# Raw weights in two pieces, later ranks behind the last mixing, rows of units asked for at any step, and a Gram rate of 1.4 in the first two mixings

## The chip, the cores and the metric

The program runs on one core of one Trainium2 chip. The metric is the device time of one execution in microseconds. The engines are named as in the profile: PE (TensorE, matmuls), PEld (its weight loads), DVE (VectorE), ACT (ScalarE), POOL (GpSimd) and SP (SyncE). SP and POOL mostly issue transfers here; "SPq" and "POOLq" are the rows in which they do so.

## What is computed

Four batches of column-normalised attention are followed by a top-1 mixture of experts over all tokens. B = 4, N = 5056, C = 256, E = 8 experts, F = 1024.

```python
qn = q / (norm(q, axis=1) + 1e-6);  kn = k / (norm(k, axis=1) + 1e-6)
s  = kn.T @ qn / tau                       # per batch: 256 x 256, summed over 5056 rows
a  = softmax(s)
x  = (v @ a).reshape(20224, 256)
e  = argmax(x @ w_gate);  p = softmax(x @ w_gate)[e]
eom = sigmoid(x @ w_output_gate)
out = p * eom[e] * (relu(x @ w1[e]) @ w2[e])   # each token by its own expert e
```

## The kernel before, in words

**Stages.** For each batch there is a *Gram* (`gram(b)`, 20 steps of 256 rows: one `qk` tile of two 256 KB loads on SP, squares on ACT L353, their sum on DVE L354, the fp32 products `s_ps` on PE L366), whose tail turns norms and products into the softmax matrix. Then comes a *mixing* (`mix(b)`, 20 turns): v is loaded on SP (L465), transposed on PE (`vt_ps` L477), split into a high and a low part (`vh` on ACT L481, `vl` on DVE L483), and multiplied by the matrix in three products (`x_ps` L506 to L508). ACT copies the result with its gate logits into a tile `st` (L509). Each group of 1024 tokens (5 groups a mixing) is *routed*: DVE finds the best expert (one-hot `r_oh` L556), PE counts by matmuls (`r_ps` L576, L579), DVE makes slot numbers (`r_si` L591), and POOL scatters the eight rows of tokens of each partition into a sorted scratch `xs_d` in DRAM, eight indirect DMAs a group (L598).

**Ranks and weights.** After two mixings the experts are ranked by how many tokens they have (`checkpoint`, whose `ri` holds the rows of rank r's weights). `prep` then loads the raw fp32 weights of each rank on SP, 1 MB for w1 (half 0, L273) and 1 MB for w2 (half 1, L276), at most DEEP = 2 halves ahead. `split` takes the root mean square of a half (ACT squares L297 and one matmul `w_ps` L301), writes fp16 high and low parts (ACT L310, DVE L311) and stores them to a scratch `wsc` (L316). Rank 0 is split right into `wbuf`. Raw tiles of ranks 0 and 1 are of their own tag "raw"; those of ranks 2 to 7 lie in the pool of `st`, four buffers that the routed rows use too, so a raw load into one waits until the scatters that read it are done.

**Units.** The expert layers run in units of 256 (later 128) slots of one expert, in order of rank: units 0 to 3 are rank 0, unit 4 is the first that may be of rank 1, unit 11 the first of rank 2. For each unit POOL fetches w1 and w2 with indirect DMAs into one of two `wbuf` slots (`fetch_w` L825, 1 MB each), SP fetches the rows (`fetch_x` L843, into the six `qk` buffers), `prepare` scales and splits them (DVE L863, ACT L880, DVE L881) and SP transposes them with two DMAs a unit (L885). PE makes h (L919 to L921, 48 matmuls), ACT and DVE split it (L923, L924), PE makes y (L942 to L944, 48 matmuls), ACT scales it (L948) and POOL scatters the rows to the output (L954). `blocks` yields after each quarter of a unit, with the y of the unit before beside the h of this one.

**What sets the order.** The program interleaves these generators by rates (`_steps`): so many steps of the second generator for each step of the first. The framework then schedules the instructions on each engine by a simulated timeline, so a changed rate, tile or number of DMAs moves instructions on every engine. Within an engine, and within SP's and POOL's issue streams, the order is fixed in the program: an instruction that waits holds up all behind it. GRATE is the number of Gram steps for each mixing step, REST the pauses before a half is split, MRATE and WRATE the steps of `prep` for each step of the last mixing and of the units behind it.

## Time and profile before

| what | value |
|---|---|
| median of 3 runs | 1206.93 us (1206.85 to 1208.63) |
| the profiled execution's own time | 1209.88 us |
| its span on the core | 1208.1 us |
| mean granted PE clock | 0.99 |
| PE, DVE, ACT, POOL busy | 1174.4, 748.5, 602.3, 517.9 us |
| HBM read, written | 281.84 MB, 61.41 MB |

The span falls into stages: Gram 0 until about 60 us, mixings 0 and 1 beside Grams 1 to 3 until about 255 us, mixing 2 beside the first units until about 355 us, the last mixing beside units until about 450 us, units alone until about 1190 us. In a view of waits a line reads "engine, instruction, what it waited for: us in all, times, longest". In a view of windows the columns are the length and then busy us and count of PE, PEld, DVE, ACT and POOL, the granted clock, the DMA share and GB/s. In a timeline the first number is the start, the second the length, and brackets hold the idle time of the engine ahead of it with what ended it. In a chain of waits each row is a start, a length and what took that time.

### The profile page before, as it was taken

The page shows a single profiled execution, that of the slowest core. Times are in us where ns is not written, and L with a number is a line of the kernel's source. Part 1 is how long each engine was busy: PE and PEld are TensorE (multiplying, and loading weights), DVE is VectorE, ACT ScalarE, POOL GpSimd, SP SyncE. Part 2 cuts the span into 40 slices and gives each one's busy share as a digit, 9 for nine tenths or more (in the row PEclk, how much of TensorE's full clock was granted, in tenths as well). Part 3 has the DMA queues.
Part 4 walks back from the last instruction along what each step waited for, and adds up shares of the span by engine and source line. Part 5 has one row for each costly group of instructions (what it writes and reads, how often), then busy time and mean ns, then how long its engine had stood idle before and what let it go on. Part 6 is the DMA issues. An engine that isn't in the chain of part 4 may idle for free.

```text
span 1208.1 us, 28097 instructions
## 1 busy us (share of the span) xinstructions
PE 1174.4 (97%) x10412; PEld 1066.4 (88%) x10412; DVE 748.5 (62%) x2300; ACT 602.3 (50%) x1193; POOL 517.9 (43%) x518
## 2 busy tenths in 40 slices
PE   8999999997997999999999999999999999999997
PEld 7899999887996888888888888888889999999997
DVE  7787768788685966566666654555554555555531
ACT  6576656576574555555556443333333444344432
POOL 0003756536565753333444433344444444444433
PEclk9999999998998999999999999999999999999999
DMA  9976888877767898657554436643325534336533
GB/s 319 330 246 207 301 277 259 295 242 215 212 242 236 223 264 178 150 147 174 148 137 126 112 80 113 182 76 77 72 63 176 112 73 82 79 81 197 168 104 130
DMA packets 186307, 208.56 MB, mean 173 GB/s; under 512 B 121832, under 2 KB 134510, under 8 KB 182200
## 3 DMA queue, kind: packets, MB, share of 16 engines
q1 hardware_dynamic: 145368, 139.41, 42.0%
q0 software_dynamic: 40512, 67.05, 18.9%
q8 instruction: 84, 1.38, 0.5%
q14 instruction: 55, 0.45, 0.1%
q10 hardware_dynamic: 288, 0.26, 0.1%
HBM read 281.84 MB, written 61.41 MB: 284 GB/s over the span
## 4 chain that ended last, share of the span: by engine, by line
PE 87%; DMA 6%; DVE 2%; issue 2%; ACT 1%; SPq 1%; POOL 0%; POOLq 0%; DVEq 0%; ACTq 0%
PE h_ps L919 11%; PE h_ps L921 11%; PE h_ps L920 11%; PE y_ps L942 11%; PE y_ps L943 11%; PE y_ps L944 11%; PE s_ps L366 10%; PE x_ps L506 3%; PE x_ps L508 2%; PE x_ps L507 2%; PE vt_ps L477 2%; DMA wbuf<-wsc,wi 1%; DMA qk<-in_k_dram 1%; DMA raw<-in_moe_w_dram 1%; DMA qk<-in_q_dram 1%
## 5 line engine op out<-in xcount | busy, mean ns | idle before, releaser
L924 DVE SCALAR_TENSOR_TENSOR hb<-h_ps,hb 128x512 f16<-128x512 f32 (+1 forms) x360 | 228.5, 636 | 276.0 <-ACT hb L923 275.1
L923 ACT ACTIVATE hb<-h_ps 128x512 f16<-128x512 f32 (+1 forms) x360 | 197.9, 552 | 364.1 <-PE h_ps L921 362.5
L919 PE MATMUL h_ps<-xt,wbuf 128*128 128x256 f16 (+1 forms) x1440 | 366.5, 262 | 3.0 <-ACT st L509 3.0
L921 PE MATMUL h_ps<-xt,wbuf 128*128 128x256 f16 (+1 forms) x1440 | 366.6, 262 | 0.0
L920 PE MATMUL h_ps<-xt,wbuf 128*128 128x256 f16 (+1 forms) x1440 | 366.5, 262 | 0.0
L942 PE MATMUL y_ps<-wbuf,hb 128*128 128x256 f16 x1296 | 353.3, 273 | 5.0 <-ACT yo L948 2.4
L944 PE MATMUL y_ps<-wbuf,hb 128*128 128x256 f16 x1296 | 353.3, 273 | 0.0
L943 PE MATMUL y_ps<-wbuf,hb 128*128 128x256 f16 x1296 | 353.3, 273 | 0.0
L825 POOL DMA_INDIRECT wbuf<-wsc,wi x172 | 177.8, 1034 | 404.5 <-PE h_ps L921 365.2
L598 POOL DMA_INDIRECT xs_d<-st,r_si x160 | 168.1, 1051 | 199.2 <-DVE r_d L550 101.9
L954 POOL DMA_INDIRECT out_dram<-yo,b_id x162 | 165.4, 1021 | 69.2 <-issue 42.3
L366 PE MATMUL s_ps<-qk 128*128 128x256 f32 x640 | 152.4, 390 | 5.8 <-DMA qk<-in_q_dram 3.9
L920 PEld LDWEIGHTS <-wbuf 128*128 128x128 f16 x1440 | 141.0, 98 | 16.9 <-issue 3.2
L919 PEld LDWEIGHTS <-wbuf 128*128 128x128 f16 x1440 | 142.1, 99 | 14.1
L921 PEld LDWEIGHTS <-wbuf 128*128 128x128 f16 x1440 | 141.1, 98 | 13.3
L943 PEld LDWEIGHTS <-hb 128*128 128x128 f16 x1296 | 126.8, 98 | 19.3 <-issue 5.6
L366 PEld LDWEIGHTS s_ps<-qk 128*128 128x128 f32 x640 | 121.4, 196 | 21.2 <-DMA qk<-in_k_dram 3.9
L944 PEld LDWEIGHTS <-hb 128*128 128x128 f16 x1296 | 126.8, 98 | 14.9
L942 PEld LDWEIGHTS <-hb 128*128 128x128 f16 x1296 | 126.8, 98 | 14.3
L354 DVE TENSOR_TENSOR acc<-acc,sq 128x1024 f32<-128x1024 f32 x76 | 92.9, 1223 | 46.8 <-ACT sq L353 45.4
L880 ACT ACTIVATE xr<-xg,b_sx 128x256 f16<-128x256 f32 x162 | 74.6, 502 | 66.8 <-DVE b_sx L233 46.4
L353 ACT ACTIVATE sq<-qk 128x1024 f32<-128x1024 f32 x76 | 80.3, 1060 | 53.0 <-DMA qk<-in_k_dram 44.8
(191 smaller groups left out, 1448.8 us busy)
## 6 DMA issues: line engine op xcount, KB each, us to landing
xg<-xs_d SPq DMA_DIRECT2D x72, 272.0 KB
qk<-in_q_dram SPq DMA_DIRECT2D x75, 256.0 KB
qk<-in_k_dram SPq DMA_DIRECT2D x75, 256.0 KB
v<-in_v_dram SPq DMA_DIRECT2D x32, 512.0 KB
raw<-in_moe_w_dram SPq DMA_DIRECT2D x16, 1024.0 KB
wsc<-whi SPq DMA_DIRECT2D x14, 512.0 KB
wsc<-wlo SPq DMA_DIRECT2D x14, 512.0 KB
v<-in_v_dram SPq DMA_DIRECT2D x8, 480.0 KB
```

What stands on the lines that cost most here:

```text
L366: nc.tensor.matmul(s_ps[:, c, :], kt[:, 1, t, c * P : (c + 1) * P], qt[:, 0, t, :], start=st == 0 and t0 == 0 and t == 0 and c == 0 and n ...
L598: ins = nc.gpsimd.indirect_dma_start(out=xs_d[:, :], out_offset=bass.IndirectOffsetOnAxis(ap=si[:np_, t : t + 1], axis=0), in_=st[:np_, t, ...
L825: nc.gpsimd.indirect_dma_start(out=wbuf[half][:, at_of(u), :], out_offset=None, in_=wsc[half][:end, :], in_offset=bass.IndirectOffsetOnAxi ...
L919: nc.tensor.matmul(hp, w1s[:, 0, c, fs], xh, start=fi == 0 and c == 0, stop=False, **KWM)
L920: nc.tensor.matmul(hp, w1s[:, 0, c, fs], xl, start=False, stop=False, **KWM)
L921: nc.tensor.matmul(hp, w1s[:, 1, c, fs], xh, start=False, stop=fin, **KWM)
L923: nc.scalar.activation(hh, h_ps[:, :, :w], AF.Relu)
L924: nc.vector.scalar_tensor_tensor(out=hb[:, 1, 2 * fp : 2 * fp + 2, :w], in0=h_ps[:, :, :w], scalar=0.0, in1=hh, op0=ALU.max, op1=ALU.subtract,
L942: nc.tensor.matmul(y_ps[:, t, :], hb[:, 0, f, tsl], w2s[:, 0, f, :], start=st, stop=False, **KWM)
L943: nc.tensor.matmul(y_ps[:, t, :], hb[:, 0, f, tsl], w2s[:, 1, f, :], start=False, stop=False, **KWM)
L944: nc.tensor.matmul(y_ps[:, t, :], hb[:, 1, f, tsl], w2s[:, 0, f, :], start=False, stop=fin, **KWM)
L954: ins = nc.gpsimd.indirect_dma_start(out=out[:, :], out_offset=bass.IndirectOffsetOnAxis(ap=un["id"][:, t : t + 1], axis=0), in_=un["yo"][ ...
```

## The change

Six things change.

1. In the first two mixings the next Grams run at 1.4 steps to a mixing step in place of 1.3 (AHEAD_RATE); the third mixing keeps 1.3.
2. Each raw half is loaded in two pieces of 512 KB, with a yield behind each (32 loads in place of 16).
3. Raw pieces of ranks 2 to 7 lie in the buffers of v (tag "v", four of them) and no longer in those of `st`.
4. Each half's high and low parts are stored in four transfers of 256 KB, each pair right behind the split of its piece (64 stores in place of 32).
5. The pause before a split (REST) is 1 in place of 2, and 4 (SLOW) for ranks 2 and later, `pause(2)` stands between the ranks 1 and 2, and WRATE is 1.0 in place of 0.8.
6. `blocks` asks for rows of units (`fetch_x`) at each step, and not only at the start of a unit.

```diff
-    GRATE = 1.3
+    GRATE, AHEAD_RATE = 1.3, 1.4
-    DEEP, LAG, REST = 2, 3, 2
+    DEEP, LAG, REST, SLOW = 2, 3, 1, 4
-    WRATE = 0.8
+    WRATE = 1.0
...
             if r > AHEAD:
-                raw = wk.tile([P, R, CW], F32, tag="st", name=f"raw{r}_{half}", bufs=STB)
-                raw = raw.rearrange("p r w -> p (r w)")[:, :HW1]
+                parts = [
+                    ld.tile([P, 4, C], F32, tag="v", name=f"raw{r}_{half}_{i}", bufs=VB).rearrange("p t c -> p (t c)")
+                    for i in range(2)
+                ]
             else:
                 raw = big.tile([P, HW1], F32, tag="raw", name=f"raw{r}_{half}", bufs=3)
+                parts = [raw[:, i * HW1 // 2 : (i + 1) * HW1 // 2] for i in range(2)]
+            raws.append(parts)
...
-            if half == 0:
-                nc.sync.dma_start(raw, wraw[0][bass.ds(row, P), :])
-            else:
-                rows = wraw[1][bass.ds(row, P), :].rearrange("(f a) (b d) -> (a b) f d", f=FC, d=C)
-                nc.sync.dma_start(raw.rearrange("p (f d) -> p f d", f=FC), rows)
-            raws.append(raw)
+            rows = wraw[half][bass.ds(row, P), :]
+            for i, part in enumerate(parts):
+                if half == 0:
+                    nc.sync.dma_start(part, rows[:, i * HW1 // 2 : (i + 1) * HW1 // 2])
+                else:
+                    nf = FC // 2
+                    of = rows.rearrange("(f a) (b d) -> (a b) f d", f=FC, d=C)[:, i * nf : (i + 1) * nf, :]
+                    nc.sync.dma_start(part.rearrange("p (f d) -> p f d", f=nf), of)
+                yield
...
             while len(raws) < min(n + DEEP, len(jobs)):
-                gather()
-                yield
-            yield from pause(LAG if n == 0 else REST)
+                yield from gather()
+            yield from pause(LAG if n == 0 else SLOW if r > AHEAD + 1 else REST)
...
+            for n, part in enumerate((hi, lo)):
+                nc.sync.dma_start(wsc[half][rows, n * HW1 + a.start : n * HW1 + a.stop], part[:, a])
             yield
-        for n, part in enumerate((hi, lo)):
-            nc.sync.dma_start(wsc[half][rows, n * HW1 : (n + 1) * HW1], part)
...
                 if fp == 1:
                     adv("prep", prepare, g + 1 + XP)
+                adv("x", fetch_x, got["prep"] + QKB)
...
-        _beside(mix(b) if b else first, (ahead, GRATE))
+        _beside(mix(b) if b else first, (ahead, AHEAD_RATE))
...
-    preps = prep(AHEAD, E)
+    preps = chain(prep(AHEAD, AHEAD + 1), pause(2), prep(AHEAD + 1, E))
```

Three places show how the scheduled order moves. (The rows of the kernel before have its line numbers; in the changed kernel L273 and L276 are L279 and L283, L316 is L320, L342 is L347, L598 is L603, L644 is L649, L825 is L830, L885 is L890, L954 is L959. `wsc_85` and `wbuf_155` are those of w1, `wsc_86` and `wbuf_156` those of w2.)

SP's issue stream where rank 0's raw weights are asked for, before:

```order
L342 DMA qk_15_3165<-in_q_dram 128x512
L342 DMA qk_15_3165<-in_k_dram 128x512
L268 TENSOR_LOAD ri
L273 ISA
L273 DMA raw_0_2793<-in_moe_w_dram 128x2048
L268 TENSOR_LOAD ri
L276 ISA
L276 DMA raw_1_2833<-in_moe_w_dram 128x8x256
L342 DMA qk_16_3243<-in_q_dram 128x512
```

and now:

```order
L347 DMA qk_19_3173<-in_q_dram 128x256
L272 TENSOR_LOAD ri
L279 ISA
L279 DMA raw_0_2853<-in_moe_w_dram 128x1024
L279 ISA
L279 DMA raw_0_2853<-in_moe_w_dram 128x1024
L272 TENSOR_LOAD ri
L283 ISA
L283 DMA raw_1_2931<-in_moe_w_dram 128x4x256
L283 ISA
L283 DMA raw_1_2931<-in_moe_w_dram 128x4x256
L349 DMA qk_19_3173<-in_q_dram 64x256
```

Before, four steps of the last Gram (16 to 19) were asked for behind the raw weights; now all but the rest of step 19 stand ahead of them.

SP's issue stream around the transposes of units 4 and 5 (both of tile `xr_3657`, two DMAs a unit), before, where `raw_1_5208` is rank 2's second half, in a buffer of `st`:

```order
L465 DMA v_4_2_5236<-in_v_dram 120x1024
L316 DMA wsc_85<-wlo_0_4402 128x2048
L268 TENSOR_LOAD ri
L276 ISA
L276 DMA raw_1_5208<-in_moe_w_dram 128x8x256
...
L885 DMA_TRANSPOSE xt<-xr_3657 128x4x128 x4
L316 DMA wsc_86<-whi_1_4850 128x2048
L316 DMA wsc_86<-wlo_1_4851 128x2048
L885 DMA_TRANSPOSE xt<-xr_3793 128x4x128 x4
```

and now, where the same tile is `xr_3685` and the four pieces of rank 2 are `raw_0_0` to `raw_1_1`, each in a buffer of v:

```order
L279 DMA raw_0_0_5343<-in_moe_w_dram 128x1024
L320 DMA wsc_85<-whi_0_4505 128x1024 x2
L320 DMA wsc_85<-wlo_0_4506 128x1024 x2
L279 ISA
L279 DMA raw_0_1_5344<-in_moe_w_dram 128x1024
L890 DMA_TRANSPOSE xt<-xr_3685 128x4x128 x2
L272 TENSOR_LOAD ri
L283 ISA
L283 DMA raw_1_0_5461<-in_moe_w_dram 128x4x256
...
L890 DMA_TRANSPOSE xt<-xr_3685 128x4x128 x2
L320 DMA wsc_86<-whi_1_4885 128x1024
```

The transposes of unit 4 now stand between two pieces of rank 2 and those of unit 5 behind the third; before, all four stood behind the whole second half.

POOL's issue stream around the last two groups of the last mixing (`st_3` and `st_4`), before:

```order
L825 DMA wbuf_156<-wsc_86,wi 128x4096
L825 DMA wbuf_155<-wsc_85,wi 128x4096
L598 DMA xs_d<-st_3_4888,r_si 163968x272 x8
L825 DMA wbuf_156<-wsc_86,wi 128x4096
L954 DMA out_dram<-yo,b_id 20224x256 x2
L825 DMA wbuf_155<-wsc_85,wi 128x4096
L598 DMA xs_d<-st_4_5247,r_si 163968x272 x8
L825 DMA wbuf_155<-wsc_85,wi 128x4096
L644 DMA xs_d<-void,tb_ei 163968x272
L644 DMA xs_d<-void,tb_ei 20496x2176
L825 DMA wbuf_156<-wsc_86,wi 128x4096
```

and now:

```order
L830 DMA wbuf_155<-wsc_85,wi 128x4096
L830 DMA wbuf_156<-wsc_86,wi 128x4096
L959 DMA out_dram<-yo,b_id 20224x256 x2
L603 DMA xs_d<-st_3_4923,r_si 163968x272 x8
L603 DMA xs_d<-st_4_5259,r_si 163968x272 x8
L830 DMA wbuf_156<-wsc_86,wi 128x4096
L830 DMA wbuf_155<-wsc_85,wi 128x4096
L959 DMA out_dram<-yo,b_id 20224x256 x2
L649 DMA xs_d<-void,tb_ei 163968x272
L649 DMA xs_d<-void,tb_ei 20496x2176
L830 DMA wbuf_155<-wsc_85,wi 128x4096
```

The first fetch of `wbuf_156` behind `st_3` is unit 5's w2 in both. Before, it stood behind eight scatters (those of `st_3`); now it stands behind sixteen.

More of the change, by code (lines that the diff above doesn't have):

```diff
@@ L296, in split @@
             a = slice(i * HW1 // 2, (i + 1) * HW1 // 2)
-            nc.scalar.activation(hi[:, a], raw[:, a], AF.Square, accum_out=ss[:, i : i + 1])
+            nc.scalar.activation(hi[:, a], raw[i], AF.Square, accum_out=ss[:, i : i + 1])
             yield
@@ L305, in split @@
         root2(tot, KW, sw, invw[:, half, r : r + 1])
-        src, dh, dl = raw, hi, lo
-        cuts = [(slice(None), slice(i * HW1 // 2, (i + 1) * HW1 // 2)) for i in range(2)]
-        for i, a in enumerate(cuts):
-            nc.scalar.activation(dh[a], src[a], AF.Copy, scale=sw)
+        for i in range(2):
+            a = slice(i * HW1 // 2, (i + 1) * HW1 // 2)
+            nc.scalar.activation(hi[:, a], raw[i], AF.Copy, scale=sw)
             nc.vector.scalar_tensor_tensor(
-                out=dl[a], in0=src[a], scalar=sw, in1=dh[a], op0=ALU.mult, op1=ALU.subtract
+                out=lo[:, a], in0=raw[i], scalar=sw, in1=hi[:, a], op0=ALU.mult, op1=ALU.subtract
             )
+            for n, part in enumerate((hi, lo)):
+                nc.sync.dma_start(wsc[half][rows, n * HW1 + a.start : n * HW1 + a.stop], part[:, a])
             yield
-        for n, part in enumerate((hi, lo)):
-            nc.sync.dma_start(wsc[half][rows, n * HW1 : (n + 1) * HW1], part)
         if half == 1:
```

## The prediction, made before the changed kernel was run

> **What bounds the kernel now.** I read the page's busy times first, then a table of windows by stage, then PE's waits, and at each wait the chain and the timeline there.
>
> ```profile
> PE 1174.4 (97%) x10412; PEld 1066.4 (88%) x10412; DVE 748.5 (62%) x2300; ACT 602.3 (50%) x1193; POOL 517.9 (43%) x518
> ```
> ```profile
> 0.00:60.00 60.00, 54.16 (x240) 47.16 (x241) 42.07 (x62) 35.77 (x36) 2.72 (x19) 0.97 0.95 325
> 60.00:210.00 150.00, 149.52 (x1052) 139.95 (x1052) 111.96 (x279) 101.78 (x206) 69.92 (x64) 1.00 0.80 258
> 210.00:255.00 45.00, 40.91 (x271) 37.71 (x270) 32.45 (x116) 27.61 (x58) 19.41 (x20) 0.96 0.83 280
> 255.00:300.00 45.00, 37.84 (x292) 35.56 (x291) 38.26 (x153) 28.82 (x68) 24.96 (x27) 0.92 0.77 227
> ...
> 355.00:385.00 30.00, 22.44 (x182) 19.98 (x182) 16.70 (x73) 14.33 (x31) 16.52 (x17) 0.89 0.78 241
> 385.00:450.00 65.00, 63.36 (x588) 56.79 (x587) 50.86 (x189) 34.46 (x64) 42.51 (x41) 1.00 0.88 230
> 450.00:1170.00 720.00, 719.75 (x6975) 649.64 (x6974) 406.73 (x1243) 314.37 (x629) 298.75 (x291) 1.00 0.50 122
> ```
>
> PE is the bound: it is busy in 97% of the span and in 719.75 of the 720 us from 450 on. The change takes no matmul away, so it can gain only where PE stands still or runs at a lower clock, and that is between 210 and 450 us: 4.1 us idle from 210 to 255, 7.2 from 255 to 300, 7.6 from 355 to 385, 1.6 from 385 to 450. The clock adds to it:
>
> ```profile
> 243.00:246.40 3.40, 3.40 (x17) 2.77 (x14) 0.43 (x4) 2.78 (x7) 0.00 (x0) 0.50 0.83 315
> 287.30:294.20 6.90, 5.14 (x31) 5.15 (x32) 5.03 (x29) 3.48 (x11) 5.38 (x6) 0.51 0.63 165
> 369.20:372.70 3.50, 2.93 (x12) 2.75 (x13) 0.97 (x6) 0.51 (x1) 1.68 (x2) 0.51 1.08 200
> 379.50:383.00 3.50, 3.16 (x15) 2.43 (x15) 1.02 (x4) 1.55 (x6) 0.88 (x2) 0.51 0.55 173
> ```
>
> Each longer stop is followed by a spell at half clock, 3.4 us or 6.9 us long, which costs half its length: 1.7 or 3.4 us. PE's waits name the stops:
>
> ```profile
> PE r_ps L576 <- DVE r_oh L556: 5.3, 1, 5.3
> PE r_ps L576 <- ACT st L509: 4.6, 2, 4.1
> PE h_ps L919 <- ACT st L509: 3.0, 1, 3.0
> PE y_ps L942 <- DMA wbuf<-wsc,wi: 1.9, 2, 1.6
> ```
>
> **Part 1, rank 0's raw weights (Gram rate, pieces): -5.** The 4.1 us wait is in the chain here:
>
> ```profile
> 231.09 8.47 DMA raw<-in_moe_w_dram
> 239.59 2.19 ACT wbuf L297 x4
> 242.83 0.19 PE r_ps L576
> ```
>
> ACT's squares of the raw half stand ahead of the copies of x that a routing needs, and the half landed at 239.6, so PE's routing matmul came at 242.8. Loss: 4.1 us idle and 1.7 us of half clock, 5.8. In the new order the Grams run ahead, the ranks are known about as early (the routing that they rest on ends 1.8 us of PE work sooner), and the first `w_ps` comes 12 us of PE work later (246.2 against 234.2 when I add up PE's matmuls in both orders, each at its own kind's duration). The weights then land some 8 us before ACT's squares. The wait goes, and I leave 0.8 us for a remainder: -5. Two pieces in place of one cost SP one more issue, which nothing waits for. Grams at 1.4 ask for 10 steps of 512 KB in about 23 us, some 220 GB/s beside v and the scatters; the profile moved 325 GB/s in its first 60 us, so between 0 and 3 us of late `qk` tiles: +1, nearer to nothing because mixings 0 and 1 ran at 258 GB/s.
>
> The Trainium skill ("DMA: Bandwidth & Descriptors", Bandwidth) says to batch transfers to 1 MiB or more; by its fit of 2.0 us plus bytes over 436 GB/s a half in two pieces takes 6.4 us in sequence and 4.4 us in one, an estimate of +2 us if the pieces don't overlap. No row here has a raw load alone; the 8.47 us are among other loads.
>
> **Part 2, DVE before unit 0: 0.** The 5.3 us wait is DVE, saturated from 262 to 289 (38.26 of the 45 us from 255 to 300): routing, unit rows, rank 0's low parts and the last Gram's tail share it.
>
> ```profile
> 288.87 0.14 DVE r_oh L556
> 289.06 0.24 PE r_ps L576
> ```
>
> By the orders, DVE's work from the second one-hot of mixing 2 to the late one sums to 45.6 us before and 42.5 now, and the PE work beside it to 36.9 and 29.3. DVE falls behind by 13.2 us in place of 8.7. Against that the one-hot before it comes 4 to 5 us earlier against PE, since PE's Gram work moved ahead of it. The lag ends at 8 to 9 us again: 0, between -4 (the head start grows by as much as the gap) and +5 (no head start).
>
> **Part 3, rank 2's second half (buffers of v, pieces): -9.5.**
>
> ```profile
> 337.91 0.39 SPq L316 DMA_DIRECT2D wsc<-wlo  x1
> 358.11 0.39 SPq L276 DMA_DIRECT2D raw<-in_moe_w_dram  x1
> ...
> 360.39 9.85 SPq L885 DMA_TRANSPOSE xt<-xr  x4
> 370.34 0.53 SPq L316 DMA_DIRECT2D wsc<-whi  x1
> ```
> ```profile
> SPq L276 <- DMA xs_d<-st,r_si: 18.5, 2, 9.4
> ```
> ```profile
> 371.62 0.51 ACT L880 ACTIVATE xr<-xg,b_sx 128x256 f16<-128x256 f32 x1 [7.06 <-DMA xt<-xr]
> 377.33 1.06 ACT L297 ACTIVATE whi<-raw 128x1024 f16<-128x1024 f32 x1 [1.19 <-DMA wsc<-whi]
> ```
>
> For 20 us SP issued nothing: the load needed a buffer of `st` whose scatters were under way. Behind it stood the transposes of units 4 and 5 and rank 1's store. ACT then stopped 7.1 us for the transposed tile, 1.2 for the store, and PE waited twice for ACT's copies (the rest of the 4.6, and the 3.0). Loss from 355 to 385: 7.6 us idle and 2 x 1.7 of clock, 11.0. Now the raw pieces wait for buffers of v, which PE's transposes free at 313 to 340 us of PE work, and unit 4's two transposes go out after the second piece (about 321), unit 5's after the third (about 331), landing at 337 to 339. ACT wants that buffer at about 335, so some 2 us of ACT's wait stay and 1.5 reach PE: -9.5 (between -11 and -6; at the low end the third piece waits one buffer longer).
>
> **Part 4, unit 5's w2 on POOL: +10.4.** Here the change adds a wait.
>
> ```profile
> 384.13 0.20 PE L576 MATMUL r_ps<-r_oh,tri 128*128 128x64 bf16 x1
> ```
> ```profile
> 385.78 1.02 POOL L598 DMA_INDIRECT xs_d<-st,r_si  x1 [1.94 <-DVE r_si L591]
> ...
> 396.55 1.05 POOL L825 DMA_INDIRECT wbuf<-wsc,wi  x1 [0.30 <-PE h_ps L921]
> ...
> 404.50 1.94 POOL L598 DMA_INDIRECT xs_d<-st,r_si  x1 [0.30 <-issue]
> ```
> ```profile
> L598 POOL DMA_INDIRECT xs_d<-st,r_si x160 | 168.1, 1051 | 199.2 <-DVE r_d L550 101.9 <-issue 40.8 <-ACT st L509 18.0
> ```
> ```profile
> 417.37 5.52 DMA wbuf<-wsc,wi
> ```
> ```profile
> 430.00:450.00 20.00, 20.00 (x186) 17.94 (x185) 13.30 (x37) 12.00 (x22) 7.75 (x9) 1.00 1.04 275
> ```
>
> Eight scatters took 385.78 to 396.55; a scatter is 1.05 us (168.1 over 160) and a gap of 0.30, so sixteen take 21.6. They start 1.7 us after the routing matmuls of `st_3` (384.13 to 385.78), and w2 lands 5.5 us after its issue: 28.8 us from those matmuls. Between them and unit 5's first y PE has, in the new order, 174 unit matmuls and 12 of x, as many as in the 20.00 us of the last row, and one routing and one `w_ps`, 0.6: 20.6 us. PE stops for 8.2 us (h of unit 6 is queued behind that y), between 6.2 (if x and the copies behind it take 2 us longer) and 9.5 (two scatters of 1.94). The clock then falls for 3.4 or 6.9 us, at 1.7 or 3.4: I take 2.2. Before, w2 stood behind eight scatters and was in time. In exchange unit 6's w2 and its 1.9 us of waits are better placed: -1.9.
>
> The Trainium skill ("TensorE: Matmul & The Clock Gate", Why this matters for your kernels) warns of PE gaps over about 3 us, after which the clock is halved until a busy window of 3.4 us. By it the price here is 1.7 and the sum -5.5. The 5.3 us stop above was followed by 6.9 us, the 4.1 us stop by 3.4, so the trace bears out the rule, not always its length.
>
> **Parts that cost nothing:** 64 stores in place of 32 and requests for rows at each step are SP issues of 0.3 to 0.5 us; from 450 us on DMA is at a share of 0.50 and rows are prepared five to six units ahead, which hides them. Without that cover a late transposed tile would cost PE what ACT's 7.1 us cost. Ranks 2 to 7 come 10 to 60 us later, far ahead of their first units.
>
> **Sum:** -5 + 1 + 0 - 9.5 + 10.4 - 1.9 = -5.0. The profiled span of 1208.1 becomes 1203.1, its own time of 1209.88 about 1204.9. That execution lies 2.95 us above the median 1206.93, so the median becomes about 1202.
>
> **The rivals.** 0.2% (2.4 us) is about what a measurement of this kernel can tell from no change.
>
> *No stall at unit 5's y.* If PE is late by 8 us or more between `st_3` and that y (the copies on ACT, or a remainder of Part 3), the fetch is in time: Part 4's 10.4 goes, 1191.5. For it: ACT was the last releaser in two of the four waits above. Against it: POOL is queued behind 16 scatters with no other engine in the way.
>
> *The gains are eaten before unit 0.* With Part 2 at +5 and no better cover for DVE the sum is 0, 1207. For it: the DVE work beside 36.9 us of PE work must now fit beside 29.3. Against it: the head start.
>
> *Slower: w2 of unit 5 behind slow scatters and a slow fetch.* A scatter of 1.94 us is in the rows above, and a fetch elsewhere took longer:
>
> ```profile
> 754.93 11.69 DMA wbuf<-wsc,wi
> ```
>
> Sixteen scatters at 1.66 (between) cost 5 us more, such a fetch 6.2: the stop is 19.4 us, and with 3.4 of clock the sum goes from -5.0 to +7.4, 1214.3. It decides where stop and clock together pass 15.4, which eats all gains. For it: two fetches and sixteen scatters share POOL's queue while SP moves raw weights. Against it: the same queue gave 5.52 at 417.
>
> *It doesn't do what it says:* SP is held by v's buffers as long as by those of `st`. Part 3 then gives 0 and the time is 1211.5, with the slower case. Against it: those buffers come free by PE's transposes, which have their data.
>
> **How the numbers follow.** Forecast, 0.46: 1202, own range 1197 to 1207 (4 off by Part 2's and 1.5 by Part 3's lower ends at most; 5 on by Part 2 or 3.5 by Part 3). No stall, 0.22: 1191.5. Gains eaten, 0.14: 1207. Slower, in either of its two forms, 0.18: 1211 to 1215. Two tenths may be left out, on the upper side half of the slower cases: the range is 1189 to 1212. Faster (below 1204.5): 0.36 of the forecast, 0.22, 0.03 of the eaten: 0.61. Same: 0.10, 0.10 and 0.01: 0.21. Slower (above 1209.3): 0.01 and 0.17: 0.18.
>
> **What would show it.** Part 1: no gap in PE near 240 us and full clock there. Part 2: the wait for `r_oh` still 4 to 6 us, before unit 0. Part 3: no SP row with 20 us of silence between 330 and 370, and ACT's wait for `xt` under 3 us. Part 4: a new PE wait of about 8 us for `wbuf`, directly after sixteen scatters. Steady part: the same length from unit 12 to the end, within 2 us. The forecast is wrong if PE's idle time moves to a place not named here, above all if `s_ps` waits for `qk` between 100 and 250 us, or if PE has idle time after 450.

## The result

The changed kernel took 1214.6 us (median of 20 runs, 1209.2 to 1220.4) against 1207.8 us (median of 20 runs of the kernel before on the same chips, 1205.2 to 1212.6). The ratio, worked out over all runs and not from the two medians, is 1.0056, with a 95% interval of 1.0043 to 1.0069: slower by 0.56%, where 0.4% faster was forecast. The profiled execution has a span of 1214.7 us against 1208.1, so the 6.6 us between the two profiles stand for the difference of the medians, 6.8.

The spread of single runs grew from 7 to 11 us. Each profile is one execution, and a stage's loss in it can be a few us off the usual one; which wait ended last in that execution is read more surely.

### The profile page after: what moved, and what is told of

It reads as the page before. It is cut to its first block, busy times and chain, and to the rows that moved or that the text cites. A ratio compares the mean times of both kernels' runs of the same rounds, so it can differ in the third digit from the quotient of the medians.

```text
span 1214.7 us, 28213 instructions
## 1 busy us (share of the span) xinstructions
PE 1177.6 (97%) x10412; PEld 1068.4 (88%) x10412; DVE 745.8 (61%) x2300; ACT 603.2 (50%) x1193; POOL 523.2 (43%) x518
## 4 chain that ended last, share of the span: by engine, by line
PE 81%; DMA 6%; DVE 4%; issue 3%; ACT 3%; POOL 2%; SPq 1%; POOLq 0%; ACTq 0%; DVEq 0%
PE h_ps L924 11%; PE h_ps L925 11%; PE h_ps L926 11%; PE y_ps L947 11%; PE y_ps L949 11%; PE y_ps L948 11%; PE s_ps L371 6%; DMA xs_d<-st,r_si 2%; PE x_ps L511 2%; PE x_ps L513 2%; PE x_ps L512 2%; PE vt_ps L482 1%; POOL xs_d L603 1%; DVE acc L359 1%; DMA qk<-in_k_dram 1%
## 5 line engine op out<-in xcount | busy, mean ns | idle before, releaser
L830 POOL DMA_INDIRECT wbuf<-wsc,wi x172 | 176.5, 1026 | 412.2 <-PE h_ps L926 369.1
L603 POOL DMA_INDIRECT xs_d<-st,r_si x160 | 170.1, 1063 | 192.8 <-DVE r_d L555 95.9
L959 POOL DMA_INDIRECT out_dram<-yo,b_id x162 | 170.1, 1050 | 71.7 <-issue 39.2
L371 PE MATMUL s_ps<-qk 128*128 128x256 f32 x640 | 149.5, 386 | 5.3 <-DMA qk<-in_q_dram 3.9
L949 PEld LDWEIGHTS <-hb 128*128 128x128 f16 x1296 | 127.3, 98 | 15.2
L511 PE MATMUL x_ps<-ah,vh 128*128 128x272 f32 x320 | 103.6, 326 | 10.8 <-ACT st L514 10.5
```

Source lines behind the costliest of these rows:

```text
L371: nc.tensor.matmul(s_ps[:, c, :], kt[:, 1, t, c * P : (c + 1) * P], qt[:, 0, t, :], start=st == 0 and t0 == 0 and t == 0 and c == 0 and n ...
L603: ins = nc.gpsimd.indirect_dma_start(out=xs_d[:, :], out_offset=bass.IndirectOffsetOnAxis(ap=si[:np_, t : t + 1], axis=0), in_=st[:np_, t, ...
L830: nc.gpsimd.indirect_dma_start(out=wbuf[half][:, at_of(u), :], out_offset=None, in_=wsc[half][:end, :], in_offset=bass.IndirectOffsetOnAxi ...
L949: nc.tensor.matmul(y_ps[:, t, :], hb[:, 1, f, tsl], w2s[:, 0, f, :], start=False, stop=fin, **KWM)
L959: ins = nc.gpsimd.indirect_dma_start(out=out[:, :], out_offset=bass.IndirectOffsetOnAxis(ap=un["id"][:, t : t + 1], axis=0), in_=un["yo"][ ...
```

## The profile after

I read the stages by the same windows as before. First the one row of the kernel before that the prediction left out, then the changed kernel's rows (length; busy us and count of PE, PEld, DVE, ACT, POOL; granted clock; DMA share; GB/s).

```profile
300.00:355.00 55.00, 54.78 (x494) 51.08 (x493) 41.15 (x175) 34.83 (x82) 30.07 (x30) 1.00 0.73 232
```
```profile
210.00:255.00 45.00, 41.99 (x270) 38.22 (x268) 31.36 (x114) 23.68 (x45) 25.10 (x21) 1.00 0.85 287
255.00:300.00 45.00, 39.65 (x319) 38.28 (x320) 40.84 (x162) 34.73 (x81) 26.20 (x26) 0.89 0.77 208
300.00:355.00 55.00, 49.21 (x431) 45.07 (x430) 37.69 (x165) 31.51 (x73) 30.16 (x31) 1.00 0.80 245
355.00:385.00 30.00, 24.19 (x190) 21.74 (x188) 18.18 (x64) 15.14 (x35) 15.94 (x17) 0.89 0.79 220
385.00:450.00 65.00, 60.58 (x547) 53.53 (x546) 45.74 (x181) 30.57 (x59) 41.30 (x40) 0.95 0.78 201
450.00:1170.00 720.00, 720.00 (x6973) 649.93 (x6972) 407.45 (x1258) 315.75 (x631) 300.47 (x289) 1.00 0.50 125
```

PE's loss in a window is its idle time (length less busy) plus what the clock costs (length times one less the clock). By that, before and after:

| window, us | before | after | difference |
|---|---|---|---|
| 210 to 255 | 4.1 + 1.8 = 5.9 | 3.0 + 0 = 3.0 | -2.9 |
| 255 to 300 | 7.2 + 3.6 = 10.8 | 5.4 + 4.9 = 10.3 | -0.5 |
| 300 to 355 | 0.2 | 5.8 | +5.6 |
| 355 to 385 | 7.6 + 3.3 = 10.9 | 5.8 + 3.3 = 9.1 | -1.8 |
| 385 to 450 | 1.6 | 4.4 + 3.3 = 7.7 | +6.1 |
| sum | 29.4 | 35.9 | +6.5 |

From 450 on PE is busy without a break in both. That the sum comes so near to 6.6 is partly chance: from 0 to 60 us the changed kernel lost 2.4 us less, a spell at half clock counts twice where PE stood still in it, and matmuls that stand wider apart count as busy. A second count avoids this: I give each matmul the median distance to the next one for its kind, over all traces of this document, add these up as PE's work, and call the time less that work PE's *lag*. It differs by -0.5 us up to 210, -2.7 from 210 to 300, +6.5 from 300 to 360, -1.7 from 360 to 390 and +5.1 from 390 to 450, 6.7 in all. So the changed kernel is not behind at 210 us, and the difference arises between 210 and 450. PE's waits name new places:

```profile
PE x_ps L511 <- ACT st L514: 10.5, 4, 4.5
PE y_ps L947 <- DMA wbuf<-wsc,wi: 4.4, 1, 4.4
PE s_ps L371 <- DMA qk<-in_q_dram: 3.9, 1, 3.9
PE vt_ps L482 <- DVE vl L488: 2.8, 1, 2.8
PE at_ps L422 <- ACT s_sb L413: 2.7, 1, 2.7
```

The waits for rank 0's raw weights (4.1) and for `r_oh` (5.3) are gone. The third row is at the start of the program and was there before. The last is the tail of the last Gram, at 276 to 279 us. The others are four places, in order of time (the first row is two of them).

**Unit 0's rows, 246 to 255 us.** ACT, then POOL, of the changed kernel:

```profile
254.81 1.78 ACT L885 ACTIVATE xr<-xg,b_sx 128x256 f16<-128x256 f32 x4 [9.01 <-DVE b_sx L233]
```
```profile
245.66 0.61 POOL L620 DMA_DIRECT2D mark<-xs_d  x1 [5.38 <-DMA xs_d<-st,r_si]
```

and the same two places of the kernel before:

```profile
259.74 0.91 ACT L880 ACTIVATE xr<-xg,b_sx 128x256 f16<-128x256 f32 x2
```
```profile
242.07 0.61 POOL L615 DMA_DIRECT2D mark<-xs_d  x1 [5.66 <-DMA xs_d<-st,r_si]
```

Unit 0's rows may be read only behind the mark, which POOL issues when the scatters of mixing 1 have landed. The mark came 3.6 us later than before, while ACT was free for unit 0's preparation at 245.8 (254.81 less 9.01) and came to it only at 259.7 before. ACT stood for 9.0 us with the copies of x queued behind it, and PE stopped for 4.1 us.

**Units 4 to 7, 330 to 346 us.** DVE of the changed kernel and of the one before:

```profile
331.51 0.17 DVE L864 COPY b_id<-xg 128x2 int32<-128x2 int32 x1 [1.85 <-DMA xg<-xs_d]
```
```profile
334.07 2.49 DVE L311 SCALAR_TENSOR_TENSOR wlo<-raw,wsw,whi 128x1024 f16<-128x1024 f32 x2
...
337.43 0.17 DVE L859 COPY b_id<-xg 128x2 int32<-128x2 int32 x1 [0.55 <-DMA xg<-xs_d]
```

Before, DVE split rank 1's weights first and prepared units 4 and on behind that. Now it waits for those rows at 331.5, prepares four units and then splits; PE's transposes (`vt_ps`) waited 2.8 us for `vl` at 346.

**The transposes of units 4 and 5, 360 to 377 us.** SP, then ACT:

```profile
353.11 0.34 SPq L279 DMA_DIRECT2D raw<-in_moe_w_dram  x1
360.38 2.54 SPq L890 DMA_TRANSPOSE xt<-xr  x2
363.99 0.41 SPq L283 DMA_DIRECT2D raw<-in_moe_w_dram  x1
364.94 0.34 SPq L848 DMA_DIRECT2D xg<-xs_d  x1
365.39 3.32 SPq L890 DMA_TRANSPOSE xt<-xr  x2
```
```profile
370.02 0.51 ACT L885 ACTIVATE xr<-xg,b_sx 128x256 f16<-128x256 f32 x1 [3.65 <-DMA xt<-xr]
...
375.55 0.51 ACT L885 ACTIVATE xr<-xg,b_sx 128x256 f16<-128x256 f32 x1 [3.77 <-DMA xt<-xr]
```

The long silence of SP is gone, but the transposes still went out at 360.4 and 365.4, as late as before (360.39). Rank 2's second piece had waited for a buffer of v until 353.1, and the third went out at 364.0 without a wait. In between, unit 4's transposes waited 7 us for PE:

```profile
SPq L890 <- PE r_ps L584: 10.7, 2, 7.1
```

The tile `xt` has the tag "vl", so it shares four buffers with the `vl` of the mixing, which PE's products of x free. The transposes then landed late: ACT got the tiles 9.6 and 10.2 us after the first issue of each pair. ACT waited 7.4 us in two parts in place of 7.1 in one.

**Unit 5's w2, 406.7 us.** POOL, and PE's chain there:

```profile
387.35 0.97 POOL L603 DMA_INDIRECT xs_d<-st,r_si  x1 [1.38 <-DVE r_si L596]
...
407.85 1.00 POOL L603 DMA_INDIRECT xs_d<-st,r_si  x1 [0.30 <-ACT yo L953]
409.15 1.09 POOL L830 DMA_INDIRECT wbuf<-wsc,wi  x1 [0.30 <-issue]
```
```profile
409.15 2.20 DMA wbuf<-wsc,wi
411.40 0.37 PE y_ps L947
```

Sixteen scatters took 387.35 to 409.15, 21.8 us (21.6 in the prediction). The fetch landed 2.2 us after its issue, not 5.5, and PE waited 4.4 us; the clock fell during the stop:

```profile
409.50:416.30 6.80, 4.90 (x24) 3.49 (x24) 3.91 (x15) 2.19 (x2) 5.27 (x6) 0.50 0.62 211
```

## The experiments

Each kernel's time is compared with runs of the kernel before on the same chip. A kernel has 4 (e8) to 20 runs, and the ratio can differ from that of the medians by 0.1%. The loss is that of the table above, in four stages, from each run's profile. Some expectations give a stage's loss from the spacing of PE's matmuls, which is 0.5 to 4 us above that. The losses of a row don't add up to its time: e5's are 22.6 against 29.1 before, and its time is the same. PE's lag at 450 us does follow the spans: 40.6 before, 47.3 changed, 40.2 for e3, 40.4 for e5 and 35.5 for e11, with spans of 1208.1, 1214.7, 1207.1, 1208.2 and 1203.4.

| kernel | median us | ratio to before (95%) | 210-300 | 300-360 | 360-390 | 390-450 |
|---|---|---|---|---|---|---|
| before | 1207.8 | 1 | 16.4 | 0.2 | 10.9 | 1.6 |
| changed | 1214.6 | 1.0056 (1.0043 to 1.0069) | 13.4 | 5.8 | 9.1 | 7.7 |
| e1 no asking at each step | 1217.8 | 1.0091 (1.0056 to 1.0127) | 15.0 | 6.6 | 4.8 | 15.2 |
| e2 rate 1.3 | 1210.5 | 1.0034 (1.0012 to 1.0057) | 9.5 | 5.3 | 4.6 | 8.6 |
| e3 raw in st | 1207.5 | 0.9996 (0.9976 to 1.0017) | 15.8 | 8.1 | 1.2 | 1.6 |
| e4 only rate 1.4 | 1212.7 | 1.0040 (1.0014 to 1.0067) | 19.4 | 0.0 | 14.4 | 2.5 |
| e5 rate 1.3, st, no asking | 1208.8 | 1.0001 (0.9988 to 1.0015) | 10.5 | 2.9 | 2.0 | 7.2 |
| e6 as e5, whole loads | 1212.9 | 1.0041 (1.0025 to 1.0056) | 13.3 | 3.7 | 0.7 | 13.9 |
| e7 as e5, one yield | 1211.4 | 1.0024 (1.0007 to 1.0040) | 16.0 | 2.1 | 1.4 | 8.1 |
| e8 as e5, raw in v | 1217.6 | 1.0077 (1.0050 to 1.0104) | 11.8 | 4.9 | 5.0 | 13.5 |
| e9 as e5, outputs later | 1207.1 | 0.9992 (0.9974 to 1.0009) | 10.0 | 4.1 | 1.8 | 6.8 |
| e10 as e5, units behind rank 1 | 1205.3 | 0.9991 (0.9973 to 1.0009) | 9.3 | 1.5 | 3.4 | 7.0 |
| e11 both | 1204.5 | 0.9981 (0.9966 to 0.9997) | 11.9 | 1.5 | 2.9 | 7.9 |

### e1: rows asked for at the start of a unit again

```diff
                     adv("prep", prepare, g + 1 + XP)
-                adv("x", fetch_x, got["prep"] + QKB)
```

> The changed kernel with one part undone: rows of units are asked for only at the start of a unit again. By the order, POOL then issues unit 5's w2 behind the eight scatters of st_3 and ahead of those of st_4; up to 325 us of PE work nothing else moves. Theory A (unit 5's w2 waits for POOL, which is busy with sixteen scatters from 387.4 to 409.2): the 4.4 us wait of PE and the 6.9 us at half clock behind it go, PE's loss between 390 and 420 us falls from 7.2 to under 1, and the time falls by about 7, to 1207.5; the 9.0 us wait of ACT for unit 0's rows stays. Rival B (the fetch itself is slow beside the pieces and quarter stores): the wait stays at 4 us or more although the fetch is issued 10 us earlier, and the time stays within 2 us of 1214.6.

Unit 5's w2 went out at 395.4 and nobody waited for it. But the time did not fall. PE's longest wait was now for unit 7's w1, which stood behind the scatters of `st_4` and the two voids:

```profile
PE h_ps L924 <- DMA wbuf<-wsc,wi: 10.1, 1, 10.1
```
```profile
412.86 1.08 POOL L649 DMA_INDIRECT xs_d<-void,tb_ei  x1 [0.30 <-DVE hb L929]
414.24 0.98 POOL L649 DMA_INDIRECT xs_d<-void,tb_ei  x1 [0.30 <-issue]
415.53 1.04 POOL L830 DMA_INDIRECT wbuf<-wsc,wi  x1 [0.30 <-issue]
```

Theory A was right on the cause of that one wait and wrong on the time: the wait moved to another fetch and grew. Rival B, a slow fetch in the old place, is out. But in the new place the landing counts: this fetch took 8.6 us to land, 6.4 more than the one of the changed kernel, and that is most of the 10.1.

### e2: the Gram rate back at 1.3

```diff
-    GRATE, AHEAD_RATE = 1.3, 1.4
+    GRATE, AHEAD_RATE = 1.3, 1.3
```

> The changed kernel with the Gram rate of the first two mixings back at 1.3. By the order, unit 0's preparation moves back behind 2.6 us of PE work on ACT, the first w_ps stays late (242 us of PE work, 233 before the change), and POOL issues unit 5's w2 between the scatters of st_3 and st_4. Theory A (the rate put unit 0's rows ahead of their mark, and by a shift of the order the w2 behind sixteen scatters): ACT's 9.0 us wait for b_sx falls under 4 and PE's 4.2 us stop with its 6.9 us at half clock behind it goes (-6 to -8); the 7.2 of unit 5's y goes too; rank 0's raw weights are not waited for, since the later w_ps comes from the pieces and not from the rate. Time 1198 to 1202. Rival B (the rate is what hid rank 0's raw weights): the wait for raw returns with 4 us and its half clock, time 1206 to 1208.

The first half of Theory A held: ACT's longest wait for `b_sx` fell from 9.0 to 3.8, PE had no long wait for rank 0's raw weights, and the loss from 210 to 300 fell to 9.5. The second did not: w2 of unit 5 was in time, but w1 of unit 6 was now the one behind the sixteenth scatter.

```profile
PE h_ps L924 <- DMA wbuf<-wsc,wi: 5.3, 1, 5.3
```

The time, 1210.5, missed both theories' ranges (1198 to 1202, 1206 to 1208).

### e3: raw pieces of ranks 2 to 7 in the buffers of st

```diff
-                parts = [
-                    ld.tile([P, 4, C], F32, tag="v", name=f"raw{r}_{half}_{i}", bufs=VB).rearrange("p t c -> p (t c)")
-                    for i in range(2)
-                ]
+                raw = wk.tile([P, R, CW], F32, tag="st", name=f"raw{r}_{half}", bufs=STB)
+                raw = raw.rearrange("p r w -> p (r w)")[:, :HW1]
+                parts = [raw[:, i * HW1 // 2 : (i + 1) * HW1 // 2] for i in range(2)]
```

> The changed kernel with the raw pieces of ranks 2 to 7 in the buffers of st again (two pieces of one tile), all else as changed. By the order, the transposes of units 4 and 5 and rank 1's second stores then stand ahead of rank 2's raw loads on SP, and unit 6's h stands ahead of unit 5's y on PE. Theory A (the raw pieces wait for buffers of v and hold the transposes behind them on SP, as the st buffers did): ACT's two waits of 3.7 us for xt and PE's loss of 9.9 between 360 and 390 go down to under 3 (-7); unit 5's y comes 5.2 us of PE work later, so its wait goes as well (-7); unit 0's wait stays. Time about 1200. Rival B (any buffer blocks SP, st for 18 us as before the change): the loss only moves behind 375 us, to units 6 and 7, and the time is 1207 or more.

This one edit takes the whole loss back. The stage from 360 to 390 lost 1.2 us:

```profile
360.00:390.00 30.00, 28.83 (x262) 26.35 (x261) 19.85 (x81) 18.39 (x41) 19.38 (x20) 1.00 0.88 267
```

The transposes went out ahead of rank 2's loads, though not sooner:

```profile
364.91 6.63 SPq L889 DMA_TRANSPOSE xt<-xr  x4
```

Again PE set the time. By that count they left at 328.8 us of PE's work, and at 328.9 in the changed kernel. What differs is the landing: ACT had unit 4's tile 6.1 us after the first issue (9.6 in the changed kernel) and did not wait for unit 5's. That the raw pieces lengthen it, by sharing the DMA engines, fits the rows and is not shown apart from the rest. No fetch was waited for long, and by the order unit 6's h stood ahead of unit 5's y. Theory A's places held. Its sum (1200) did not: unit 0's wait stayed (9.6 us of ACT), as it said, but the stages from 210 to 360 lost 4.7 us more than in the changed kernel. The time is in rival B's range (1207 or more), though the loss did not move behind 375 us as B said. The edit moves the order on PE and POOL too, so its gain is not the price of the buffers alone.

### e4: the rate 1.4 alone, on the kernel before

```diff
-        _beside(mix(b) if b else first, (ahead, GRATE))
+        _beside(mix(b) if b else first, (ahead, 1.4))
```

> The kernel before with one part of the change alone: the first two mixings run with 1.4 Gram steps to a step. By the order, unit 0's preparation comes 2.6 us of PE work earlier on ACT, as in the changed kernel; units 4 and 5 have their transposes around rank 2's second half, and unit 5's w2 stays behind eight scatters. Theory A (the rate trades the wait for rank 0's raw weights against one for unit 0's rows): ACT waits 7 to 10 us for unit 0's rows, PE's loss between 210 and 300 us is 16 to 19 us (20.0 before, 17.3 in the changed kernel), the time 1203 to 1207. Rival B (the rate is a loss by itself, also through q and k that come late): over 1209, with s_ps waiting for qk. Rival C (it is most of the gain that was forecast): under 1202.

```profile
256.34 0.91 ACT L880 ACTIVATE xr<-xg,b_sx 128x256 f16<-128x256 f32 x2 [10.03 <-DVE b_sx L233]
```

The rate alone is a loss of 0.4%. ACT waited 10 us for unit 0's rows, as Theory A said, and the loss from 210 to 300 rose to 19.4, that from 360 to 390 to 14.4. The time is above A's range and in B's (over 1209); q and k were not late, so B's second half is out. Rank 0's raw weights, loaded whole here, were not waited for by PE, and by ACT for 2.2 us at most: the rate removes that wait too.

### e5 to e8: what pieces, yields and buffers do at rate 1.3

e5 undoes three parts at once: rate 1.3, buffers of st, rows at the start of a unit (the diffs of e1 to e3). Pieces, quarter stores and pauses remain.

> The changed kernel with three parts undone: the Gram rate is 1.3, the raw pieces of ranks 2 to 7 lie in the buffers of st, rows are asked for at the start of a unit. The pieces, the quarter stores and the new pauses remain. By the order, unit 0's preparation is where it was before the change, the transposes of units 4 and 5 are ahead of rank 2's loads, and POOL issues w1 of unit 6 and w2 of unit 5 between the scatters of st_3 and st_4. Theory A (each of the three parts carries its own loss): PE loses 15 to 16 us between 210 and 300 (as with the rate alone undone), 7 to 9 between 300 and 360, about 3 between 360 and 390 and under 4 from there to 450; about 7 to 9 less than before the change in all, time 1198 to 1200. Rival B (a place freed in the last mixing is filled by the next fetch that POOL issues late, whichever it is): a wait of 4 us or more for wbuf between 390 and 430, time 1204 or more.

e6 loads each half whole and keeps both yields:

```diff
-            for i, part in enumerate(parts):
-                if half == 0:
-                    nc.sync.dma_start(part, rows[:, i * HW1 // 2 : (i + 1) * HW1 // 2])
...
-                yield
+            if half == 0:
+                nc.sync.dma_start(raw, wraw[0][bass.ds(row, P), :])
...
+            yield
+            yield
```

> As the run before (rate 1.3, buffers of st, rows at the start of a unit), but each raw half is loaded whole by one transfer of 1 MB, with the two yields of the two pieces kept, so that the order stays nearly the same (first w_ps at 242 us of PE work). Theory A (rank 0's raw wait went because the yields put ACT's squares later in the order, not because of smaller transfers): no raw wait of PE near 240 us, the time within 2 us of the run with pieces. Rival B (pieces land sooner, and that is what helped): PE's 4 us wait and its half clock return, time 4 to 6 us above the run with pieces.

e7 keeps the pieces and yields once for a half:

```diff
-                yield      # in the loop over the two pieces
+            yield          # behind the loop
```

> As the run with pieces in st at rate 1.3, but with one yield for a half in place of one for each piece. By the order, the first w_ps is at 233 us of PE work, as before the change, and ACT's squares of rank 0 stand ahead of the copies for the routing again. Theory A (the place of the squares decides): PE waits 2 to 4 us near 238, its clock falls there, 4 to 6 us more between 210 and 255 than with the run with pieces; time 3 to 6 us above it. Rival B (pieces help by themselves): no such wait.

e8 is e5 with the edit of e3 taken back: the raw pieces lie in the buffers of v, as in the changed kernel.

> As the run with pieces in st at rate 1.3, but with the raw pieces of ranks 2 to 7 in the buffers of v, as the change has them. By the order, the transposes of units 4 and 5 stand between rank 2's pieces on SP again, and POOL issues w1 of unit 6 ahead of the scatters of st_4, w1 of unit 7 and w2 of unit 6 behind them and the two voids. Theory A (the buffers of v hold the transposes, and the order on POOL then makes unit 7's h wait): ACT waits over 3 us for xt at 365 to 375, PE loses 5 to 7 between 360 and 390, and unit 7's h waits 7 to 10 us for w1; time 9 to 16 us above the run with pieces in st. Rival B (v's buffers are no worse than those of st at this rate): within 3 us.

e5 kept all that was expected up to 390 us and lost it behind that: PE waited 5.0 us for unit 7's w1. By the count of lag it was 5.6 us ahead of the kernel before at 390 and gave 5.4 of that back by 450. Rival B was right, and the time stayed at 1.0001.

e6 against e5 overturns my account of rank 0's wait. The first `w_ps` came as late in e6 as in e5 (258.3 and 259.2 us), yet PE waited 4.0 us again. ACT's first square, in e5 and then in e6:

```profile
239.12 1.06 ACT L302 ACTIVATE wbuf<-raw 128x1024 f16<-128x1024 f32 x1 [4.79 <-DMA raw<-in_moe_w_dram]
```
```profile
237.14 1.06 ACT L300 ACTIVATE wbuf<-raw 128x1024 f16<-128x1024 f32 x1 [7.56 <-DMA raw<-in_moe_w_dram]
```

The first square waits for 512 KB in e5 and for 1 MB in e6, and in e5 a copy of x stands between two squares. So at this rate the loads in pieces removed the long wait, not the place of `w_ps`; whether by the earlier landing or by the copy that now stands between the squares, these runs don't separate. e7 agrees: with `w_ps` back at an early place (248.4) the longest wait of PE there, near 240, was 1.7 us, not 4. Its loss of 5.5 us more than e5's lies elsewhere, at 270 to 300 (13.0 against 7.6), where neither theory looked. The Trainium skill ("DMA: Bandwidth & Descriptors", Bandwidth) advises transfers of 1 MiB or more; it speaks of throughput, and here the first consumer's wait decided, 4.8 us against 7.6. The 2 us that the prediction estimated for two pieces in sequence don't show: ACT had the whole half 8.4 us after its issue (228.72), and both pieces within 7.5 of the first's (233.09).

e8 against e5 gives the price of v's buffers at this rate: the stage from 360 to 390 loses 5.0 in place of 2.0, and unit 7's h waits 8.4 us for its w1. Theory A held on both, but ACT's waits for xt were 2.4 us at most, not over 3.

### e9 to e11: POOL in the last mixing

The table's last column gave a new theory: that POOL is a second bound there, and that whatever was gained earlier comes back as a wait for some fetch between 390 and 450. POOL's busy time from 390 to 420 is the same in all of these, of before, changed, e5 and e11:

```profile
390.00:420.00 30.00, 30.00 (x285) 26.93 (x283) 28.73 (x123) 16.63 (x29) 23.59 (x22) 1.00 0.80 217
```
```profile
390.00:420.00 30.00, 25.58 (x222) 22.02 (x220) 24.07 (x114) 9.83 (x20) 23.39 (x22) 0.89 0.65 184
```
```profile
390.00:420.00 30.00, 24.61 (x211) 21.08 (x210) 23.79 (x102) 10.94 (x19) 23.29 (x23) 0.94 0.89 232
```
```profile
390.00:420.00 30.00, 25.40 (x211) 21.54 (x209) 21.13 (x77) 11.91 (x22) 23.49 (x20) 0.89 0.82 209
```

About 20 to 23 issues of 1.05 to 1.2 us with a gap of 0.30 behind each fill the 30 us. From 389 to 417 us POOL has no gap above 0.52 in any of the thirteen traces, in the kernel before as well, whose PE was 5.6 us behind e5's by then and found its fetches nearly in time.

e9 moves the outputs of units 3 to 5 behind the fetch of unit 7's w1:

```diff
-        nc.gpsimd.indirect_dma_start(
+        units[u]["f%d" % half] = nc.gpsimd.indirect_dma_start(
...
-            if g > a + 1:
+            if g == 7:
+                with tc.issue_after(units[7]["f0"].ins):
+                    for u in (3, 4, 5):
+                        store(u)
+            elif g > a + 1 and g not in (5, 6):
                 store(g - 2)
```

> As the run with pieces in st at rate 1.3, with one thing moved on POOL: the outputs of units 3, 4 and 5 are issued behind the fetch of unit 7's w1, which then follows directly on the scatters of st_4. PE's order and all else on SP, DVE and ACT stay. Theory A (in the last mixing POOL is busy without a break from the scatters of st_3 to the fetch of unit 7's w1, and whatever PE has gained before comes back as a wait for that fetch): w1 of unit 7 is issued about 4 us earlier (two outputs took 405.1 to 409.1), PE's wait of 5 us for it falls to 1 to 2 and the half clock behind it goes or shrinks: 4 to 6 us less between 390 and 420, time about 1203 to 1204. Rival B (the fetch is slow to land because SP's raw loads, stores and transposes share the DMA engines): the wait stays at 4 us or more although the issue is earlier, and the time stays at 1208.

Unit 7's w1 was now in time, and PE waited for unit 6's w2, the next fetch behind two outputs:

```profile
PE y_ps L946 <- DMA wbuf<-wsc,wi: 5.1, 2, 4.5
```
```profile
409.38 0.99 POOL L958 DMA_INDIRECT out_dram<-yo,b_id  x1 [0.30 <-issue]
410.67 1.05 POOL L829 DMA_INDIRECT wbuf<-wsc,wi  x1 [0.30 <-issue]
```

Moving one pair moved the wait, which is what a POOL without free time would give. But the landing is a second cause. PE wanted this w2 at 414.6, 3.9 us after its issue, and it took 8.4 to land; unit 7's w1 had landed in 2.4. The two in the chain, and the windows of both landings:

```profile
406.02 2.38 DMA wbuf<-wsc,wi
...
410.67 8.43 DMA wbuf<-wsc,wi
```
```profile
406.00:408.40 2.40, 2.40 (x24) 2.15 (x23) 2.40 (x9) 1.45 (x2) 2.08 (x2) 1.00 0.51 164
410.70:419.10 8.40, 3.90 (x36) 3.33 (x35) 3.23 (x20) 1.65 (x4) 6.57 (x7) 0.97 1.10 269
```

In the second, SP's raw pieces, stores and transposes were under way too, as rival B had it. In eight kernels the fetch that PE waited for longest is one of two kinds. Three landed 2.1 to 3.7 us after their issue (changed, e2, e11; DMA share 0.24 to 0.68) and were late by POOL's queue. Five took 6.6 to 8.6 us (e1, e5, e6, e8, e9; share 1.03 to 1.11). With a landing of 2.2 us PE would have waited about 0.6 in e5 and not at all in e6 and e9, by my estimate from these rows, and some 3.7 in e1 and e8. So POOL as the bound is not shown: the wait is made by its queue and by landings beside SP's transfers, and no run here takes the two apart. The time did not improve clearly (0.9992).

e10 holds the preparation of unit 4, and by the order that of units 5 to 7, on DVE behind the split of raw weights that is the latest in the program at that point (`last_lo`):

```diff
-            nc.vector.scalar_tensor_tensor(
+            last_lo[0] = nc.vector.scalar_tensor_tensor(
...
+        with tc.issue_after(last_lo[0].ins) if u == 4 else ExitStack():
-        copied = nc.vector.tensor_copy(idt[:, :nt], xr[:, :, C])
+            copied = nc.vector.tensor_copy(idt[:, :nt], xr[:, :, C])
```

> As the run with pieces in st at rate 1.3, with the preparation of units 4 to 7 held on DVE behind a split of raw weights, so that by the order it comes at 315 to 322 us of PE work on ACT (298 to 306 in the run with pieces, 310 to 317 before the change). Theory A (the change put these preparations ahead of work that PE needs, and their rows come only behind the second mark, so that DVE and ACT wait in order): PE's loss between 330 and 360 falls from 4.9 to about 2, the time by up to 3; but the gain may come back at POOL's fetch of unit 7's w1, as the wait there is the last one. Rival B (these losses come from the split of rank 1 in the same place): the loss between 330 and 360 stays at 4 to 5.

> The two edits together: outputs of units 3 to 5 behind unit 7's w1 on POOL, and the preparation of units 4 to 7 held back on DVE. Theory A (POOL is the second bound of the last mixing): with the outputs out of the way, the gain of the earlier part is kept: PE loses about 2 between 330 and 360 and under 3 between 390 and 450, time 1200 to 1202, faster than the kernel before by 0.3 to 0.5%. Rival B: the losses move to another fetch (w2 of unit 6) and the time stays within 2 us of 1208.

In e10 the stage from 300 to 360 fell from 2.9 to 1.5, as Theory A said, but the next rose from 2.0 to 3.4, so that no gain is left at 390, and no change in time can be told. e11, with both edits, is the only kernel whose interval lies below 1, and only just: 0.9981 (0.9966 to 0.9997), 2.3 us faster than the kernel before (0.0019 of 1207.9, the median before in those runs). It missed its own forecast (1200 to 1202), because the last column stayed at 7.9. The fetch that PE waited for there (4.6 us) landed in 2.1, but stood behind scatters of which two took 2.7 and 2.1 us (394.46 and 400.09).

## Why the prediction was wrong, point by point

| term | forecast | measured, from the two profiles |
|---|---|---|
| Part 1, rank 0's raw weights | -5, and +1 for the Grams | the wait gone, none for `qk`; but a new wait for unit 0's rows. Parts 1 and 2 together: -3.4 |
| Part 2, DVE before unit 0 | 0 | the 5.3 us wait for `r_oh` gone; `at_ps` waits 2.7 |
| 300 to 355 us | no term | +5.6 |
| Part 3, rank 2's second half | -9.5 | -1.8 |
| Part 4, unit 5's w2, less 1.9 | +8.5 | +6.1 |
| sum | -5.0 | +6.5 |

**Part 1.** The wait went, as forecast, and the working was only half right. The prediction laid it on the Grams running ahead, with the first `w_ps` 12 us later. The rate does remove the wait, with whole loads too (e4); so do the pieces at the old rate (e5, e7). The late `w_ps` alone does not: e6 has it, and the wait. Nor did the weights land 8 us before ACT's squares: ACT still waited 0.8 us for the first. And the step missed what stands next on ACT: with the Grams ahead, unit 0's preparation reached ACT before its mark. So the rate, which the prediction took for the carrier of the gain, is by itself a loss (e4, 1.0040).

**Part 2.** The rival "eaten before unit 0" named the right stage but the wrong wait: not the pile of work on DVE, but rows that weren't there yet.

**Part 3 is the step that failed most**, by 7.7 us: -9.5 was forecast for the end of ACT's and PE's waits from 355 to 385, and -1.8 came. Its reading of v's buffers was right. By the count of PE's work the second and third piece left at 321.7 and 332.6 us (321 and 331 in the prediction), and ACT wanted its buffer at 335.0 (335). Two things failed. Unit 4's transposes did not leave behind the second piece but 7 us later, since `xt` needs a buffer that PE frees; the prediction didn't ask for it. And the second pair, sent at 365.4, landed 10.2 us later, where 6 to 8 was counted, so ACT waited 7.4 us in place of 2. PE then stopped for 5.8 us, not 1.5, and its clock fell for 6.8 more. The rival "it doesn't do what it says" (1211.5) had the effect right and the cause wrong: it was not v's buffers that held the transposes. With the pieces in st's buffers and rank 2's loads behind the transposes, the stage's loss is 1.2 (e3), and at rate 1.3 2.0 against 5.0 (e5 and e8). What in the landing makes that difference stays open.

**The missing term, 300 to 355.** The prediction looked for waits at the places where the trace of before had them. The order of e5 has the preparation of units 4 to 7 on ACT some 11 us of PE work earlier than before (298 to 306, not 310 to 317), ahead of rank 1's split, and the changed kernel's DVE rows show the same turn (331.51 and 337.43); nothing in the working asked what that would be queued before. e10 moves it back and halves the loss of this stage, but the next stage loses as much more. The rest of it, 3 us at 300 to 330, is there in the changed kernel and in e3, little in e1 (1.1) and not at rate 1.3, nor with the rate alone (e4); what causes it stays open.

**Part 4.** Mechanism and place were right, 21.8 us for sixteen scatters against 21.6; the landing was over-sized (2.2, not 5.5). The clock was nearly right: 6.8 us at half clock, but PE was busy for 4.9 of them, which cost about 2.5 (2.2 in the prediction). What was wrong is the view of it as one wait that the order happened to make. e5, which has gains before it and not this order, gives them back there, by a fetch behind POOL's issues that was also slow to land.

**Luck.** The measured 1214.6 lies where the rival "slower" put it (1211 to 1215). Its mechanism did not occur: the sixteen scatters came 1.36 us apart, not 1.66, and the fetch was quick.

**The trace's own sign.** All gains were taken from stages whose end is set by a chain of PE, DVE, ACT and SP, and the row of 385 to 450 us shows PE at 63.36 of 65 and POOL at 42.51 with no look at how much of POOL's rest are gaps of 0.30 between issues. Counted with them, its 41 issues take about 55 of the 65 us, and from 386 to 433 us the trace of before has no gap on POOL above 0.31.

## What to carry to other kernels

Before adding up the stalls that an edit removes, look for what PE will wait for when it arrives earlier. Count the gap behind each issue as busy: an engine shown at 78% can be full. Price a fetch with the transfers that run beside it. Work that is moved forward in an in-order queue is only worth something if what it waits for moves too; here rows of units stood behind a mark that didn't. When a buffer is changed to free one queue, work out when every buffer that the queued instructions need comes free, not only the one that was changed.

## What the runs showed of the hardware that I had not expected

An indirect fetch of 1 MB landed between 2.1 us (e11, 402.44, DMA share 0.24) and 8.6 us after its issue (e1, 415.53, share 1.03), so a single row is a poor price for it.

The spells at half clock at stops of PE of 4.1 to 4.5 us were 6.8 us long three times in the changed kernel. The Trainium skill ("TensorE: Matmul & The Clock Gate", Why this matters for your kernels) puts the limit at gaps of about 3 us. The trace agrees for these long stops only: a spell of 3.4 us also came with a stop of 2.1 us (before, 369.3) and one of 2.7 (changed, 279.8), and none with one of 2.8 (changed, 346.3). A spell can begin before the stop is over (409.5 and 411.4), and only its busy part costs.

Scatters on POOL slow down together: 1.0 us in most rows, but 1.4 to 1.9 in five of the changed kernel's between 223 and 235 us, where DMA was at a share of 0.98. POOL, and the window:

```profile
233.15 1.90 POOL L603 DMA_INDIRECT xs_d<-st,r_si  x1 [0.30 <-issue]
235.36 1.00 POOL L603 DMA_INDIRECT xs_d<-st,r_si  x1 [0.30 <-issue]
```
```profile
223.00:235.00 12.00, 12.00 (x81) 11.28 (x80) 11.62 (x32) 8.09 (x14) 10.17 (x7) 1.00 0.98 330
```

Those five took 3.7 us more than five of 1.0 would have (8.75 less 5.0), about what the mark came later (3.6). Whether the load on DMA is the cause was not tried, and slow scatters are not all that makes a mark late: e8's came at 245.3 with none of over 1.25 us behind 200 us.
